# Two constants of a planned order: precedence for tanh, gates and evacuations, and a margin behind loads

## The chip, the cores and the metric

The kernel runs on one core of a Trainium2 chip. The metric is the device time of one execution in microseconds; the kernel before has a median of 448.25 us over 13 runs (447.63 to 455.56). A core has five engines with a queue each, which work side by side: TensorE (PE in the profile: matrix products, with PEld its weight loads), VectorE (DVE), ScalarE (ACT), GpSimd (POOL) and SyncE (SP), which here issues most of the DMAs. Each takes its instructions in the order written; one that waits holds up those behind it on the same engine.

## The reference

It is a cosine attention followed by a two-layer MLP on its output, with batch 8, 12 heads, 448 positions, head width 64, model width 768 and inner width 2048:

```python
q_n = q / (norm(q) + 1e-6);  k_n = k / (norm(k) + 1e-6)
attn = softmax(q_n @ k_n.T / tau)            # tau = 0.1
x = (attn @ v)  # heads joined: 3584 tokens x 768
h = x @ w_in                                 # 768 x 2048
g = h * sigmoid(1.702 * h)
out = g @ w_out                              # 2048 x 768
```

All inputs and the output are float32 in memory; the kernel multiplies in float16.

## The kernel before

**The work.** Attention goes by head pairs x = 0 to 47, six a batch. For a pair: q, k and v are loaded (L229, 224 KB each, issued by SP); q and k are squared (L242 on ScalarE; L241 on GpSimd for pairs 6 to 11) and summed by VectorE (L248); the norms are worked out by VectorE for a group of one, two or three pairs at once (L256–L293); GpSimd scales q and k (L314) and casts v (L330). Scaled q and k are transposed, by TensorE for batches 0 and 1 (L338, L350), by a DMA from SP for batch 2 on (L355, tile qkT). TensorE makes scores (L375, or L437 in halves for batches 0 and 1; tile sp), ScalarE their exp (L386, tile et), TensorE the attend (L401, or L454), VectorE its normalisation (L412, L415), and the result is transposed into xT: from batch 2 on by a DMA from SP (L425), before that on TensorE (L477, L487).

The MLP of a batch follows. mm1 makes 16 units of 128 inner columns (L500, six matmuls each; L530 for batch 0), each followed by a tanh on ScalarE (L510) and a gate on VectorE (L517, L542), which form g from h. mm2 (L555) works on two batches together, in seven tiles of 128 tokens by two halves of the width, 16 matmuls each, the first three tiles after the even batch and the other four after the odd one. ScalarE evacuates each half (L566, tile ost) and SP stores it (L583).

**Buffers.** Small pools tie the parts together: two score buffers in PSUM (sp), one attend buffer (a, tile avp), three for the products (mm), three for tanh (th), two for squares (sq), seven each for q and k, four for v, two for the output (ost). An operation of the plan takes a buffer and a later one frees it: a gate frees the mm and th of its unit, an evacuation the mm of its half, an exp frees sp, a reduction sq, a scaling q or k, and the second step of a normalisation a.

**The order.** It isn't written by hand. Each operation is added to a `Plan` with its engine, a planned time, a due number, the operations it follows, and the buffers it takes and frees. `order` (L71) runs a small event simulation of the engines and the DMA queues and writes the instructions in the order in which they start there. When an engine of the plan comes free it takes, among the operations that are ready (all they follow has ended) and whose buffers are free, the one with the lowest due number:

```python
heapq.heappush(ready[ops[u][0]], (ops[u][2], u))      # L149: (due, index)
```

Readiness comes first, the due number only chooses among what is ready. A DMA of the plan lands when its packets have passed at a fixed rate, and those who use it, and the buffers that it frees, are ready DMA_US + SEM_US = 1.9 + 0.1 us later (L129). Planned times of ScalarE are 0.82 us for an exp, 0.53 for a square, 0.46 for a tanh, 0.40 for an evacuation. Until 50 planned us, gaps of TensorE are filled by dummy transposes (L346).

Due numbers count in half pairs. Pair x has s = 2x from batch 1 on. Its loads are due s − 13, its squares and reductions 8 before the first pair of its group, the scalings about s − 5, qkT s − 3, scores and exps s to s + 1, attends and normalisations s + 2 and s + 3, xT s + 4. The products of batch b are spread over 12(b + 1) + 9 to 12(b + 2) + 9 (from 8 on for batch 0); a product's tanh, gate, evacuation and store carry the due number of the product. Loads keep a fixed order among themselves; all of SP's work, stores and transposes too, goes through SP's one queue. The loads of batch 2 stand behind the second weight load w_out.

Of the kernel before, what the change touches and what calls it, by code (L numbers as in the profile page):

```python
# [20 lines left out]
SEM_US = 0.1  # L21
SWITCH_US = 0.12
DMA_US = 1.9
DMA_ENGINES, DMA_PKT_US, DMA_KB_US = 16, 0.024, 0.037
MOE_FROM, MOE_LAG = 8, 9
WARM_FROM, KEEP_WARM, FILL_US, FILL_SPARE = 1.5, 50.0, 0.056, 0.3
# [2 lines left out]
def packets(n, nbytes):  # L29

    one = DMA_PKT_US + DMA_KB_US * nbytes / 1024
    return n * one / DMA_ENGINES, one


class Plan:
# [6 lines left out]
    def add(self, name, eng, us, due, emit, after=(), takes=(), frees=(), dma=None, rows=128, hold=(), turn=False):  # L42
        after = list(after) + list(hold)
        if turn:
            self.turns.append((due, len(self.turns), name))
        self.ops[name] = (eng, us, due, emit, after, takes, frees, dma, rows, hold)
# [24 lines left out]
    def order(self):  # L71

        for n, (_, _, name) in enumerate(sorted(self.turns)):
            eng, us, due, emit, after, takes, frees, *more = self.ops[name]
            takes, frees = [*takes, (("turn", n), 1)], [*frees, (("turn", n + 1), 1)]
            self.ops[name] = (eng, us, due, emit, after, takes, frees, *more)
            self.free["turn", n + 1] = 0
        self.free["turn", 0] = 1
        ops = list(self.ops.values())
        index = {n: i for i, n in enumerate(self.ops)}  # L80
        left = [len(o[4]) for o in ops]
        users = [[] for _ in ops]
        for i, o in enumerate(ops):
            for a in o[4]:
                users[index[a]].append(i)
        idle = {o[0]: 0.0 for o in ops}
        ready = {e: [] for e in idle}
        for i, o in enumerate(ops):
            if not left[i]:
                heapq.heappush(ready[o[0]], (o[2], i))  # L90

        lines, moved = {}, 0.0
        events, out, now, mode = [], [], 0.0, 128
        while True:
            for e in idle:
                held = []
                while idle[e] <= now and ready[e]:
                    due, i = heapq.heappop(ready[e])
                    _, us, _, emit, _, takes, _, dma, rows, _ = ops[i]
                    if any(self.free[s] < k for s, k in takes):  # L100
                        held.append((due, i))
                        continue
                    for s, k in takes:
                        self.free[s] -= k
                    out.append((now, i, emit))
                    if e == "PE" and rows != mode:
                        mode = rows
                        us += SWITCH_US
                    idle[e] = now + us
                    heapq.heappush(events, (idle[e], i, True))  # L110
                    if dma is None:
                        heapq.heappush(events, (idle[e] + SEM_US, i, False))
                for h in held:
                    heapq.heappush(ready[e], h)
            if len(out) == len(ops):
                return out

            while True:
                heads = [q[0] for q in lines.values() if q]
                total = sum(h[1] for h in heads)  # L120
                landed = min((moved + h[0] * total / h[1] for h in heads), default=None)
                if landed is None or (events and events[0][0] <= landed):
                    break
                for h in heads:
                    h[0] -= (landed - moved) * h[1] / total
                moved = landed
                for q in lines.values():
                    if q and q[0][0] <= 1e-6:
                        heapq.heappush(events, (moved + DMA_US + SEM_US, q.pop(0)[2], False))  # L129
            if not events:  # L130
                raise RuntimeError("the plan cannot go on")
            now = events[0][0]
            for h in heads:
                h[0] -= (now - moved) * h[1] / total
            moved = now
            while events and events[0][0] <= now:
                _, i, own = heapq.heappop(events)
                eng, dma = ops[i][0], ops[i][7]
                if own and dma is not None:
                    lines.setdefault(eng, []).append([*dma, i])  # L140
                for s, k in ops[i][6]:
                    if own == (s == "port" or s[0] == "turn"):
                        self.free[s] += k
                for u in users[i]:
                    if (ops[u][0] == eng and dma is None) != own:
                        continue
                    left[u] -= 1
                    if not left[u]:
                        heapq.heappush(ready[ops[u][0]], (ops[u][2], u))  # L149
# [3 lines left out]
def kernel(  # L153
# [453 lines left out]
    add = plan.add  # L607
# [10 lines left out]
    for x in range(NPAIR):  # L618
# [3 lines left out]
        for ti, nm in ((1, "k"), (0, "q")):  # L622
            add(("load", nm, x), "ACT" if x + ti == 0 else "SP", 0.5, s - 13, partial(load, x, (q32, k32)[ti], (q, k)[ti], nm + "32"),
                takes=[(nm, 1)], dma=PAIR, hold=hold, turn=True)
            pl = sq_pool(x, ti)
            add(("sq", ti, x), "POOL" if pl else "ACT", 1.0 if pl else 0.53, early + ti * 0.1, partial(square, x, ti),
                after=[("load", nm, x)], takes=[("sq", 1), ("port", int(pl))], frees=[("port", int(pl))])
            add(("red", ti, x), "DVE", 0.6, early + 0.2, partial(reduce, x, ti),
                after=[("sq", ti, x)], frees=[("sq", 1)])
# [3 lines left out]
                after=[("norm", 1, grp)], takes=[("qks", 1), ("port", 1)], frees=[(nm, 1), ("port", 1)])  # L633
        if x == grp[0]:
            reds = [("red", ti, y) for y in grp for ti in range(2)]
            n = len(grp)
# [3 lines left out]
        if x == grp[0] and not first:  # L640
# [3 lines left out]
            takes=[("v", 1)], dma=PAIR, hold=hold, turn=True)  # L644
        ca = x in CA
        add(("cast", x), "ACT" if ca else "POOL", 0.64 if ca else 0.75, s - 0.5, partial(cast_v, x),
            after=[("load", "v", x)], takes=[("vt", 1), ("port", 1 - ca)], frees=[("v", 1), ("port", 1 - ca)])
        if x < TURN:
            add(("tp", x), "PE", 0.4, s - 3, partial(transposes, x),
                after=[("scale", 0, x), ("scale", 1, x)], takes=[("a", 1), ("qkT", 1)], frees=[("qks", 2)])  # L650
            add(("qkT", x), "DVE", 0.6, s - 3, partial(transposed, x), after=[("tp", x)], frees=[("a", 1)])
        else:
            add(("qkT", x), "SP", 1.3, s - 3, partial(dma_transposed, x),
                after=[("scale", 0, x), ("scale", 1, x)], takes=[("qkT", 1)], frees=[("qks", 2)],
                dma=packets(2 * P, C * D * 4))
        if x < HALF:
            for h in range(2):
                sh = x + HP * h if first else s + h
                for u in range(2):
                    key = (x, h, u)  # L660
                    add(("s",) + key, "PE", 0.2, sh, partial(scores_h, *key), after=[("qkT", x)] + [("s", min(x + AHEAD, HP - 1), 0, 1)] * (first and h),
                        takes=[("sp", 1)], frees=[("qkT", h * u)], rows=64)
                    add(("exp",) + key, "ACT", 0.82, sh + 0.1, partial(exp, *key), after=[("s",) + key],
                        takes=[("exp", 1)], frees=[("sp", 1)])
                es = [("exp", x, h, u) for u in range(2)] + [("cast", x)]
                add(("at", x, h), "PE", 0.48, sh + 1, partial(attend_h, x, h), after=es,
                    takes=[("mm", 1)], frees=[("exp", 2), ("vt", h)])
                add(("nx", x, h), "DVE", 0.65, sh + 1, partial(normalise_h, x, h), after=[("at", x, h)],
                    takes=[("xs", 1)])
                add(("turn", x, h), "PE", 0.15, sh + 1, partial(turn_h, x, h), after=[("nx", x, h)],  # L670
                    frees=[("xs", 1)])
                add(("x", x, h), "ACT" if x in XA and not h else "DVE", 0.35, sh + 1, partial(turned_h, x, h), after=[("turn", x, h)],
                    takes=[("x", 1 - h)], frees=[("mm", 1)])
            continue
        for c in range(C):
            add(("s", x, c), "PE", 0.19, s + c // 2, partial(scores, x, c), after=[("qkT", x)],
                takes=[("sp", 1)], frees=[("qkT", int(c == C - 1))], rows=64)
            add(("exp", x, c), "ACT", 0.82, s + c // 2 + 0.1, partial(exp, x, c),
                after=[("s", x, c)], takes=[("exp", 1)], frees=[("sp", 1)])
        for j in range(2):  # L680
            es = [("exp", x, c) for c in range(C)] + [("cast", x)]
            if j == 1:
                es.append(("nx", x, 0))
            add(("at", x, j), "PE", 0.475, s + 2 + j, partial(attend, x, j), after=es,
                takes=[("a", 1)], frees=[("exp", 4 * j), ("vt", j)])
            add(("nx", x, j), "DVE", 0.55, s + 2 + j, partial(normalise, x, j), after=[("at", x, j)],
                takes=[("xf", 1 - j)], frees=[("a", 1)])
        add(("x", x), "SP", 1.0, s + 4, partial(turn, x), after=[("nx", x, 1)],
            takes=[("x", 1)], frees=[("xf", 1)], dma=packets(256, 512))
# [5 lines left out]
    def moe_due(b):  # L695
        return 2 * HP * (b + 1) + MOE_LAG if b else MOE_FROM
# [4 lines left out]
    for b in range(B):  # L701
# [3 lines left out]
        for u in units:  # L705
            key = u if b else u + ("h",)
            m, half = u[1], not b
            after = [prev] if prev else []
# [13 lines left out]
        for t in tiles:  # L722
            for n in range(2):
                for part in range(4):
                    if b:
                        after = [("g", b, 4 * part + 3)]
                    else:
                        after = [("g", h, 4 * part + 2, "h") for h in range(1 + (t > 0))]
# [18 lines left out]
    for name, us, emit, after, takes, frees, tail in moe:  # L747
        b, part = divmod(B * done / total, 1)
        start, end = moe_due(b), moe_due(b + 1)
        due = start + (end - start) * part  # L750
        done += us
        add(name, "PE", us, due, emit, after=after, takes=takes, frees=frees)
        prev = name
        for kind, eng, n, e, tk, fr in tail:
            if eng == "SP":
                add(kind + name[1:], eng, 0.5, due, e, after=[prev], frees=fr, dma=n)
            else:
                me = (kind,) + name[1:]
                before = [prev]
                if kind == "ost":  # L760
                    me = me[:-1]
                    if me[-1]:
                        before.append(me[:-1] + (0,))
                add(me, eng, n, due, e, after=before, takes=tk, frees=fr)
                prev = me
    for i in range(2):
        add(("w_in", i), "POOL", 1.0, i - 2, partial(load_w_in, i), hold=[("load", "q", HP - 2)],
# [53 lines left out]
```

## Time and profile before

| | |
|---|---|
| median of the runs | 448.25 us |
| the profiled execution: time, span | 447.82 us, 445.7 us |
| TensorE busy (share of the span) | 427.5 us (96%) |
| ScalarE busy | 301.6 us (68%) |
| VectorE busy | 236.8 us (53%) |
| GpSimd busy | 146.2 us (33%) |
| exps L386, 192 | 166.2 us on ScalarE, 35.9 idle before them |
| tanhs L510, 128 | 69.3 us, 32.6 idle before them |
| evacuations L566, 56 | 27.4 us, 43.5 idle before them |
| squares L242, 84 | 53.1 us, 25.7 idle before them |
| gates L517 and L542, 128 | 77.8 us on VectorE |

The page is one execution on the chip. Busy times are sums over the span, so a share says little of a single stage; the stretches of 20 us are read for that. A line of the timeline gives start, length, engine, line, operation, output and inputs, the count of instructions merged into it, and in brackets the idle time of the engine before it with what ended that. Records of ScalarE that follow each other overlap: two exps of 0.92 us take 1.72 together. The ends of matmuls are modelled, so a TensorE that reads as busy may still be slower than it could be; what it costs is better read from one start to the next. Small gaps on an engine that others do not wait for cost nothing.

### The profile page before, as it was taken

Reading aid. Unit: us, or ns where it says so; the run is one execution under the profiler, and the core shown is the slowest. Engines: PE = TensorE matmul, PEld = TensorE weight load, DVE = VectorE, ACT = ScalarE, POOL = GpSimd, SP = SyncE. Lnnn points to the kernel's source line nnn. Section 1 sums busy time; section 2 is a strip of 40 time slices with the busy share of each in tenths; the row PEclk is TensorE's granted clock in tenths of the full one; section 3 lists DMA queues with packets and bytes.
Section 4 is the critical chain, followed back from the end, with each engine's and each line's share of the span. In section 5 each row is a group of like instructions: output and inputs, shape, how many; then the busy total and the mean of one; then the engine's idle time right before and its main releaser. Section 6 shows DMA issues by size and latency. Waiting matters only on the chain.

```text
span 445.7 us, 10624 instructions
## 1 busy us (share of the span) xinstructions
PE 427.5 (96%) x4208; PEld 264.3 (59%) x4208; DVE 236.8 (53%) x629; ACT 301.6 (68%) x478; POOL 146.2 (33%) x209
## 2 busy tenths in 40 slices
PE   8899999898989998999999999999999999999996
PEld 8668878454545654556555654556555655565563
DVE  4857878677697527652776228651453125504400
ACT  5898398769997759876886658865775557314411
POOL 2746776287564622433150613333110000000000
PEclk9999999999999999999999999999999999999999
DMA  8999597999999996656644795536201331021022
GB/s 214 243 223 256 98 208 180 272 268 232 223 244 202 191 223 114 165 150 169 176 113 127 191 186 135 161 97 122 69 19 26 76 84 25 13 71 37 0 72 71
DMA packets 95888, 63.99 MB, mean 144 GB/s; under 512 B 56288, under 2 KB 90848, under 8 KB 95840
## 3 DMA queue, kind: packets, MB, share of 16 engines
q1 hardware_dynamic: 91952, 56.81, 53.9%
q0 software_dynamic: 3648, 6.29, 7.8%
q8 instruction: 33, 0.54, 0.5%
q10 hardware_dynamic: 240, 0.23, 0.1%
q14 instruction: 15, 0.12, 0.1%
HBM read 45.61 MB, written 11.01 MB: 127 GB/s over the span
## 4 chain that ended last, share of the span: by engine, by line
PE 69%; ACT 9%; DVE 8%; DMA 5%; issue 3%; POOL 3%; SPq 2%; ACTq 0%; POOLq 0%
PE mm L555 27%; PE mm L500 24%; PE avp L401 6%; DMA k<-in_k_dram 5%; PE sp L375 5%; ACT et L386 5%; PE tps L346 4%; ACT sq L242 2%; DVE n L248 2%; POOL qks L314 2%; SPq L583 1%; PE sp L437 1%; PE mm L454 1%; ACT th L510 1%; PE mm L530 1%
## 5 line engine op out<-in xcount | busy, mean ns | idle before, releaser
L386 ACT ACTIVATE et<-sp 112x896 f16<-112x896 f32 x192 | 166.2, 917 | 35.9 <-PE sp L375 28.1
L555 PE MATMUL mm<-w_out,gT 128*128 128x384 f16 x896 | 153.3, 326 | 0.2 <-ACT ost L566 0.2
L500 PE MATMUL mm<-xT,w_in 128*128 128x448 f16 x672 | 134.8, 353 | 1.1 <-DVE gT L517 0.9
L555 PEld LDWEIGHTS <-gT 128*128 128x128 f16 x896 | 84.4, 98 | 65.9 <-issue 13.1
L500 PEld LDWEIGHTS <-w_in 128*128 128x128 f16 x672 | 62.7, 98 | 67.6 <-issue 13.8
L517 DVE SCALAR_TENSOR_TENSOR gT<-th,mm 128x448 f16<-128x448 f16 x112 | 68.3, 616 | 56.0 <-ACT th L510 55.8
L510 ACT ACTIVATE th<-mm 128x448 f16<-128x448 f32 x128 | 69.3, 549 | 32.6 <-PE mm L500 26.5
L248 DVE TENSOR_REDUCE n<-sq 112x8 f32<-112x512 f32 x96 | 64.1, 680 | 46.4 <-ACT sq L242 45.5
L330 POOL CAST vt<-v 112x256 f16<-112x256 f32 x92 | 35.1, 402 | 119.1 <-PE avp L401 85.5
L566 ACT ACTIVATE ost<-mm 128x384 f32<-128x384 f32 x56 | 27.4, 489 | 43.5 <-PE mm L555 42.0
L314 POOL TENSOR_TENSOR qks<-k,y 112x512 f16<-112x512 f32 x42 | 43.8, 1042 | 39.1 <-DVE y L289 26.5
L401 PEld LDWEIGHTS <-et 112*128 112x128 f16 x1152 | 44.6, 97 | 15.6 <-ACT et L386 2.0
L401 PE MATMUL avp<-vt,et 112*128 112x65 f16 x1152 | 47.4, 193 | 3.1 <-ACT et L386 1.7
L314 POOL TENSOR_TENSOR qks<-q,y 112x512 f16<-112x512 f32 x42 | 43.8, 1042 | 3.5 <-DVE y L289 3.5
L412 DVE RECIPROCAL rcx<-avp 128x4 f32<-128x4 f32 x72 | 12.9, 179 | 59.4 <-PE avp L401 59.1
L375 PE MATMUL sp<-qkT 64*128 64x448 f16 x288 | 40.8, 355 | 2.0 <-ACT et L386 1.9
L242 ACT ACTIVATE sq<-k 112x512 f32<-112x512 f32 x42 | 26.5, 632 | 21.4 <-DMA k<-in_k_dram 20.7
L415 DVE TENSOR_TENSOR xf<-avp,rcx 128x256 f16<-128x256 f32 x72 | 30.6, 424 | 2.5
L242 ACT ACTIVATE sq<-q 112x512 f32<-112x512 f32 x42 | 26.6, 638 | 4.3 <-DMA q<-in_q_dram 2.9
L346 PE MATMUL tps<-ident 128*128 128x128 f16 x288 | 20.8, 234 | 4.2 <-DVE qkT L350 2.8
L346 PEld LDWEIGHTS <-ident 128*128 128x128 f16 x288 | 18.8, 106 | 5.8 <-issue 4.4
L530 PE MATMUL mm<-xT,w_in 128*128 128x224 f16 x192 | 20.7, 259 | 0.1
(44 smaller groups left out, 212.7 us busy)
## 6 DMA issues: line engine op xcount, KB each, us to landing
k<-in_k_dram SPq DMA_DIRECT2D x48, 224.0 KB, 4.6
v<-in_v_dram SPq DMA_DIRECT2D x48, 224.0 KB, 4.7
q<-in_q_dram SPq DMA_DIRECT2D x47, 224.0 KB, 5.0
w_in<-in_moe_w_in_dram POOLq DMA_DIRECT2D x2, 1536.0 KB, 16.7
w_out<-in_moe_w_out_dram POOLq DMA_DIRECT2D x2, 1536.0 KB, 14.3
out_dram<-ost SPq DMA_DIRECT2D x7, 336.0 KB, 2.8
out_dram<-ost SPq DMA_DIRECT2D x8, 288.0 KB, 2.7
out_dram<-ost SPq DMA_DIRECT2D x8, 240.0 KB, 3.0
```

Of the source, the lines that this page charges most:

```text
L242: return nc.scalar.activation(out=sqs[x, ti], in_=src, func=AF.Square)
L248: nc.vector.tensor_reduce(out=n2s[grp][:, x - grp[0], ti], in_=sqs.pop((x, ti)), axis=AX.X, op=ALU.add,)
L314: return eng.tensor_tensor(out=qkss[x][:, 1 - ti].rearrange("p c j d -> p j c d"), in0=src, in1=rss[x][:, ti, :, :, None].to_broadcast((P, ...
L330: copy(out=vt[:, :, j, :D], in_=src[:, j]) for j in range(2)
L346: nc.tensor.transpose(out=tps0[:, 2 * S : 2 * S + 128], in_=ident, identity=ident)
L375: nc.tensor.matmul(out=sp[:, j, :S], lhsT=keys(x, j, c), rhs=queries(x, j, 0, S), start=True, stop=True,)
L386: nc.scalar.activation(out=e[:, : 2 * S].rearrange("p (j s) -> p j s", j=2), in_=sps.pop(key)[:P, :, :S], func=AF.Exp, scale=inv_tau, **kw,)
L401: nc.tensor.matmul(out=ps[:, (D + 1) * t : (D + 1) * (t + 1)], lhsT=exps[x, c][:, q0 : q0 + 128], rhs=values(x, c, D * j, D * j + D + 1), ...
L500: nc.tensor.matmul(out=ps[:, :S], lhsT=w_in_sb[:, kk, 128 * m : 128 * (m + 1)], rhs=xTs[b, kk][:, :S], start=(kk == 0), stop=(kk == KT1 - 1),)
L510: nc.scalar.activation(out=ths[key], in_=mms[key][:, :S], func=AF.Tanh, scale=0.851)
L517: nc.vector.scalar_tensor_tensor(out=gts[b // 2][:, m, (b % 2) * S : (b % 2 + 1) * S], in0=ths.pop((b, m)), scalar=1.0, in1=mms.pop((b, m) ...
L555: nc.tensor.matmul(out=mms[b2, t, n][:, :NW], lhsT=gts[b2][:, kk, 128 * t : 128 * (t + 1)], rhs=w_out_sb[:, kk, NW * n : NW * (n + 1)], st ...
```

## The change

A constant line is added, and two places use it:

```diff
+LATE_FROM, LATE_US, URGENT = 80.0, 2.0, 12
...
                     if q and q[0][0] <= 1e-6:
-                        heapq.heappush(events, (moved + DMA_US + SEM_US, q.pop(0)[2], False))
+                        at = moved + DMA_US + SEM_US + LATE_US * (moved > LATE_FROM)
+                        heapq.heappush(events, (at, q.pop(0)[2], False))
...
-                add(me, eng, n, due, e, after=before, takes=tk, frees=fr)
+                add(me, eng, n, due - URGENT, e, after=before, takes=tk, frees=fr)
```

The first: a DMA whose packets have passed after 80 planned us, a load, a transpose or a store, is taken to be usable 2 us later than so far. That changes the planned time only, and with it the place of its users in their queues; the waits on the chip stay those of the data. The second: tanh, gate and evacuation (`me` in the loop over the tails of the products) get a due number lower by 12, the width of one batch, for all batches. The due numbers of the products and of the stores stay as they are. No instruction is added, removed or changed in size.

## The prediction

> **What bounds the kernel now.** I read the chain of waits first, to learn which engine sets the end and to get its prices.
>
> ```profile
> 187.35 0.49 PE avp L401 x16
> 386.78 15.60 PE mm L555 x96
> 402.38 18.16 PE mm L500 x96
> 420.54 20.81 PE mm L555 x128
> ```
>
> TensorE sets the end, and where it is fed without a break it has fixed prices: mm2 20.81/128 = 0.163 us a matmul, mm1 18.16/96 = 0.189, attend 0.49/16 = 0.031. In the timeline, scores (L375) take about 0.48 per four and 0.30 per two up to the next matmul; I use 0.13 each. Next, the busy times by 20 us stretch say where it is not fed.
>
> ```profile
> core 0: us, PE busy (x) PEld busy (x) DVE busy (x) ACT busy (x) POOL busy (x), PEclk, DMA share, GB/s
> 80.00:100.00 20.00, 17.49 (x137) 9.72 (x137) 14.68 (x41) 13.89 (x24) 11.21 (x18) 1.00 1.12 268
> 100.00:120.00 20.00, 18.23 (x202) 9.87 (x199) 13.71 (x38) 19.99 (x32) 13.76 (x20) 1.00 1.08 240
> 120.00:140.00 20.00, 18.39 (x194) 10.47 (x190) 17.77 (x49) 19.08 (x32) 7.85 (x11) 1.00 1.02 214
> 160.00:180.00 20.00, 18.03 (x168) 10.13 (x165) 12.34 (x32) 14.14 (x24) 5.30 (x8) 1.00 0.76 156
> 260.00:280.00 20.00, 19.20 (x176) 10.61 (x174) 12.01 (x32) 15.39 (x26) 6.44 (x9) 1.00 0.65 157
> 280.00:300.00 20.00, 20.00 (x186) 11.29 (x182) 12.22 (x34) 14.73 (x24) 5.41 (x9) 1.00 0.48 129
> ```
>
> The same view for single lines gives the counts. In 280:300 they are 42 mm1, 40 mm2, 24 scores, 80 attends: 42×0.189 + 40×0.163 + 24×0.13 + 80×0.031 = 20.1 us of work in 20, so that stretch has nothing to give. In 100:120: 48×0.189 + 34×0.13 + 120×0.031 = 17.2, a loss of 2.8 us. In 120:140 (42, 20 mm2, 22, 110) 17.5, a loss of 2.5; in 160:180 (54, 16, 18, 80) 17.6, 2.4; in 260:280 (54, 22, 20, 80) 18.9, 1.1; in 80:100 I take the unbusy 2.5. **The ceiling for any order of the work after 80 us is about 11.3 us**, and the stages hit are 80–140, 160–180 and 260–280. Granted clock is 1.00 throughout.
>
> Who starves TensorE? The waits on its engine and the timeline at two of those places:
>
> ```profile
> PE sp L375 <- ACT et L386: 1.9, 3, 0.8
> PE avp L401 <- ACT et L386: 1.7, 3, 0.6
> PE mm L454 <- ACT et L386: 1.5, 2, 1.3
> ```
>
> ```profile
> 82.58 0.63 ACT L242 ACTIVATE sq<-k 112x512 f32<-112x512 f32 x1 [1.36 <-DMA k<-in_k_dram]
> 84.06 0.60 PE L454 MATMUL mm<-vt,et 112*128 112x65 f16 x14 [1.33 <-ACT et L386]
> ...
> 167.33 0.63 ACT L242 ACTIVATE sq<-k 112x512 f32<-112x512 f32 x1 [3.15 <-DMA k<-in_k_dram]
> 169.62 0.57 PE L401 MATMUL avp<-vt,et 112*128 112x65 f16 x13 [0.60 <-ACT et L386]
> ```
>
> ScalarE stood 1.36 and 3.15 us before a square whose load had not landed; the exp queued behind it came late, and TensorE waited for the exp. That is one cause. The other:
>
> ```profile
> 100.37 1.31 PE L500 MATMUL mm<-xT,w_in 128*128 128x448 f16 x6
> 101.91 1.31 PE L500 MATMUL mm<-xT,w_in 128*128 128x448 f16 x6
> ...
> 106.69 1.46 ACT L510 ACTIVATE th<-mm 128x448 f16<-128x448 f32 x3
> ```
>
> The mm1 begun at 100.37 ended near 101.7; its tanh ran at 106.69, 5 us later, behind exps and squares. All three mm buffers were held, and the next mm1 began only at 105.92, when the first gate (105.26, 0.61) had released one.
>
> **The change part by part.** No instruction is added or removed, and durations stay. Two things move.
>
> *Precedence (URGENT).* Tanh (128), gates (128) and evacuations (56) are chosen before ready exps, squares, reductions and normalisations. Stores keep their due on SP, but follow their evacuation, so may come earlier there. Queued behind an urgent instruction is everything else on ScalarE and VectorE, at 0.43 us for a tanh (next start in the timeline), 0.49 for an evacuation, 0.61 for a gate; waiting for that are attends (for exps), a second attend (it needs the single avp buffer, released by the normalise) and, through later squares, POOL's scaling and the q/k/v loads on SP that wait for those buffers.
>
> In 100–140, TensorE's two stretches lose 5.3. A tanh and its gate release 1.13 us of mm1 for 0.43 of ScalarE; four exps release about 2 us for 3.3. So putting tanh first feeds TensorE better, and the exps postponed can run beside mm2, which asks for one evacuation in 2.6 us (140–160: ScalarE busy 14.4 of 20). Against it: ScalarE is busy 39.07 of 40 there, and order creates no capacity. Bounds 0 and 5.3; I take 3.0, above half, because the timeline shows the mm buffers as the stop. In 80–100, mm waits for an evacuation twice 0.2: 0.4 gained. In 160–180, mm1 waited 0.7 for a gate at 175.95: gained.
>
> *Margin (LATE).* After 80 planned us, everything fed by a DMA is planned 2 us later: squares, casts, scores behind a transposed qkT, mm1 behind xT. The planned load is 0.5 to issue, 224 packets of 0.061 over 16 engines = 0.85, and 1.9 + 0.1: 3.35 us. The trace's landings in 80:180 and in 180:300:
>
> ```profile
> k<-in_k_dram SPq DMA_DIRECT2D x17, 224.0 KB, 4.8
> ...
> k<-in_k_dram SPq DMA_DIRECT2D x14, 224.0 KB, 3.4
> ```
>
> The Trainium skill speaks against the margin: "DMA: Bandwidth & Descriptors", in its anatomy of one DMA, fits a transfer as about 2.0 us plus its bytes at 436 GB/s (a fit for GpSimd's path), an estimate of 2.5 us for 224 KB. By that the plan already waits long enough and the margin brings 0. By the row it is 1.45 us short in 80–180, and the square at 167.33 shows the price. I go by the row: 1.33 gained at 82–84, 1.2 at 168–170 (0.63 + 0.60), 0.8 at 260–280 (ScalarE waits of 2.65, 2.42 and 1.76 for k there): 3.3. ScalarE's other waits for loads, most of its 20.7 us for k, lie beside a full TensorE and give nothing.
>
> The margin has a price. Transposes landed in a median of 4.8 (qkT) and 3.5 us (xT) in 80:180, 2.6 and 2.4 later, against planned 4.15 and 3.7: for them it is mostly too much. xT has a lag that hides it. qkT has none when batch 2 starts (first scores at 97.51; ScalarE idle 1.24 before its first exp): scores placed up to 2 us later leave ScalarE idle just before its full stage. Bounds 0 and 2; I take 1.0, as mm1 of batch 1 can fill for TensorE. SP issues in planned order, so later squares and scales also move qkT transposes behind loads; one pair of transposes held SP for 10.3 us at 168.47. This may help or hurt by under 1; I take 0.
>
> New waits: 16 tanhs lie in 97–143. If each made TensorE wait its 0.43 for an exp it would be 6.9; if none, 0. Mm1 is ready during most of them: I take 1.5. From 181 to 250 and 272 to 386 TensorE is full; reordering costs nothing there while mm1 or mm2 covers it, 0.43 a place where it doesn't. Splitting a four of scores into two twos would cost 2×0.30 − 0.48 = 0.12: zero taken, up to 2 for 16 more. Before 80 us only precedence acts, on batch 0; TensorE is full in 60–80 and partly kept warm by dummy transposes before: 0, within ±1.
>
> **Sum:** 3.0 + 0.4 + 0.7 + 3.3 − 1.0 − 1.5 = 4.9 us. The profiled execution took 447.82 (span 445.7 and 2.1 around it), 0.43 below the median of 448.25. I forecast 448.25 − 4.8 = **443.5**.
>
> **The rivals.**
> 1. *The order cuts deeper.* TensorE never starves after 97: three quarters of 11.3, 8.5, gives 439.8. For it: mm work was ready in every starved stretch. Against: ScalarE's 39.07 of 40. Chance 0.16.
> 2. *No change.* ScalarE's capacity in 100–140 decides, priorities apply only where several things are ready at once, and what is won at loads returns as late exps: 448. For it: ScalarE's share; two score buffers and two square buffers keep its ready list short. Chance 0.12.
> 3. *Slower.* In 97–143, tanhs and gates push exps and normalises back, and the margin starts batch 2's scores 2 us late; ScalarE, full, can't recover either. Price 2.0 + 16×0.43 = 8.9, against 6.0 gained elsewhere (0.4 + 0.7 + 3.3, and 1.6 of the 3.0): +2.9, 451.1. It decides once TensorE waits for the postponed exps at more than about 9 of the 16 tanhs. VectorE's 17.77 of 20 in 120:140 speaks for it; mm2 as a filler against. Chance 0.22.
>
> **How the numbers follow.** The main case has 0.50 (441 to 446.5: in 100–140 the full 5.3 at the low end, 0 at the high one). About 0.2% (0.9 us) is what a measurement can tell from no change. Faster 0.50 + 0.16 = 0.66, same 0.12, slower 0.22. A range of 438.5 to 450.5 leaves out the far halves of rivals 1 and 3.
>
> **What would show it.** Right: ScalarE's wait for k below 10 us; tanh within 1.5 us of its mm1 in 97–140 and the mm1s of batch 1 finished before 130 instead of 135; TensorE over 19 busy in 100:120, 120:140 and 160:180; the last three groups of the chain unchanged in length, only earlier by 4 to 5 us. Wrong: "avp <- ACT et" or "sp <- ACT et" above 4 us, first scores of batch 2 after 99, or a new unbusy stretch after 180, where nothing is forecast to move.

## The result and the profile after

The changed kernel takes 443.89 us (median of 11 runs), the one before 449.1 (48 runs, the 13 of the beginning among them): a ratio of 0.9885, 95% interval 0.9864 to 0.9905. The forecast was 443.5. The two profiled executions are closer: 447.82 and 444.67, spans 445.7 and 442.8. All readings below are of the profiles.

The busy times by stretch, with the columns shown before. The first line is 60–80 of the kernel before, the others are the changed kernel, whose program lines are 2 higher:

```profile
60.00:80.00 20.00, 20.00 (x317) 15.91 (x315) 16.68 (x48) 16.47 (x25) 11.53 (x18) 1.00 0.93 200
...
60.00:80.00 20.00, 17.66 (x259) 11.99 (x260) 15.22 (x46) 16.15 (x20) 11.72 (x13) 1.00 0.91 176
80.00:100.00 20.00, 18.45 (x207) 11.52 (x207) 17.62 (x52) 15.00 (x27) 10.37 (x18) 1.00 1.09 241
100.00:120.00 20.00, 20.00 (x179) 9.89 (x177) 13.73 (x37) 19.87 (x32) 10.52 (x15) 1.00 1.13 256
120.00:140.00 20.00, 20.00 (x221) 11.34 (x220) 15.25 (x41) 19.73 (x31) 11.36 (x16) 1.00 1.18 224
160.00:180.00 20.00, 18.17 (x156) 9.92 (x154) 13.23 (x34) 16.05 (x27) 12.34 (x16) 1.00 1.03 189
260.00:280.00 20.00, 20.00 (x182) 11.20 (x182) 12.51 (x33) 16.17 (x26) 6.89 (x9) 1.00 0.71 165
```

TensorE is full in 100–140 and in 260–280, as forecast; ScalarE is no less busy there than before. 160–180 is hardly better, and 60–80, which was full, is not. ScalarE's waits for k (total, times, longest) fell below the forecast 10 us, before and after:

```profile
ACT sq L242 <- DMA k<-in_k_dram: 20.7, 17, 3.2
...
ACT sq L244 <- DMA k<-in_k_dram: 7.3, 6, 2.5
```

I counted every kernel's matmuls in each stretch and took them off at the fixed prices of the prediction (batch 0 and 1's forms in the same way, 0.105 for L530, 0.034 for L454, 0.061 for L437, dummies and other transposes 0.065); a matmul across an edge counts on both sides. What remains of a stretch is its **loss**:

| kernel | median us | ratio (95%) | 60–80 | 80–100 | 100–140 | 160–180 | 260–280 |
|---|---|---|---|---|---|---|---|
| before | 449.1 | | −0.5 | 3.3 | 5.4 | 2.4 | 1.2 |
| the change | 443.89 | 0.9885 (0.9864–0.9905) | 3.7 | 2.4 | 1.9 | 1.9 | −0.1 |
| 1 precedence only | 447.48 | 0.9969 (0.9951–0.9988) | 2.2 | 4.4* | 1.9 | 2.4 | 1.3 |
| 2 margin only | 445.81 | 0.9928 (0.9894–0.9963) | −0.4 | 1.7 | 7.4* | 0.0 | −0.1 |
| 3 precedence from batch 1 | 441.50 | 0.9838 (0.9797–0.9878) | −0.6 | 2.5 | 2.1 | 1.0 | 0.0 |
| 4 margin on loads only | 443.66 | 0.9887 (0.9846–0.9929) | 3.0 | 3.7 | 1.8 | 0.1 | −0.1 |
| 5 = 3 and 4 | 441.15 | 0.9844 (0.9795–0.9893) | −0.6 | 1.4 | 2.8 | 1.2 | 0.0 |
| 6 batch 0: tanhs only | 442.47 | 0.9870 (0.9826–0.9915) | 1.4 | 2.0 | 2.1 | 0.3 | −0.1 |
| 7 batch 0: gates only | 446.81 | 0.9961 (0.9943–0.9979) | 2.8 | 7.1* | 2.1 | 0.6 | −0.1 |
| 8 from batch 1, tanhs only | 440.60 | 0.9825 (0.9784–0.9865) | −0.6 | 1.6 | 2.7 | 0.3 | 0.1 |
| 9 from batch 1, gates only | 446.60 | 0.9937 (0.9912–0.9962) | −0.5 | 2.0 | 7.8* | 0.2 | 0.0 |
| 10 = 8, margin from the start | 440.24 | 0.9801 (0.9772–0.9829) | −0.1 | 0.1 | 1.9 | 0.1 | 0.0 |
| 11 = 8 without margin | 444.49 | 0.9892 (0.9859–0.9926) | −0.4 | 1.8 | 2.6 | 2.1 | 1.2 |
| 12 = 8, margin 4 us | 440.07 | 0.9800 (0.9769–0.9830) | −0.5 | 2.0 | 2.2 | 0.0 | 0.0 |

(* the granted clock was below 1 in part of it; see the last section. Runs 1–4, 5–8 and 9–12 were timed in three groups, each beside runs of the kernel before, with medians of 448.47, 448.90 and 449.19. Between groups the ratios compare better than the medians.)

The profile's difference closes on this table. From 80 to 380 the losses fell from 12.0 to 6.4 in all (5.6 gained), and there are 34 dummy transposes fewer (2.2 gained); 60–80 lost 4.2 and the first 60 us 0.6 more. That makes 3.0, against spans that differ by 2.9. The chain of waits ends as before, with groups of the same length, 3.2 earlier:

```profile
383.62 15.60 PE mm L557 x96
399.22 18.16 PE mm L502 x96
417.38 20.82 PE mm L557 x128
```

The medians differ by 2 us more than the profiles. The granted clock may explain part. Averaged over the span it was 1.000 in before's profiled execution, and 0.996 in the middle one of 71 later runs; of those, the 22 at 0.998 or more have a median of 448.4 us, the 48 at 0.996 or less one of 449.0. The change's 0.997 is no loss: it fell at 440.54, after the last matmul (438.18). So some 0.6 is accounted for, and the rest stays open.

### The profile page after: what moved, and what is told of

The parts are those of the page before. It is cut to its first block, busy times and chain, and to the rows that moved or that the text cites. A ratio compares the mean times of both kernels' runs of the same rounds, so it can differ in the third digit from the quotient of the medians.

```text
span 442.8 us, 10584 instructions
## 1 busy us (share of the span) xinstructions
PE 426.6 (96%) x4174; PEld 262.6 (59%) x4174; DVE 240.6 (54%) x629; ACT 302.0 (68%) x478; POOL 146.1 (33%) x209
## 4 chain that ended last, share of the span: by engine, by line
PE 78%; DMA 8%; DVE 5%; ACT 3%; POOL 3%; issue 2%; SPq 1%; POOLq 0%; ACTq 0%
PE mm L557 30%; PE mm L502 28%; PE sp L377 7%; PE avp L403 7%; DMA k<-in_k_dram 4%; DMA w_in<-in_moe_w_in_dram 3%; PE mm L532 2%; POOL qks L316 2%; ACT et L388 2%; DMA qkT<-qks 1%; PE mm L456 1%; DVE n L250 1%; ACT sq L244 1%; PE sp L439 1%; DVE gT L544 1%
## 5 line engine op out<-in xcount | busy, mean ns | idle before, releaser
L348 PE MATMUL tps<-ident 128*128 128x128 f16 x254 | 19.5, 239 | 3.2 <-DVE qkT L352 1.8
L348 PEld LDWEIGHTS <-ident 128*128 128x128 f16 x254 | 17.4, 109 | 4.7 <-issue 3.3
```

The costliest lines, as they stand in the source:

```text
L348: nc.tensor.transpose(out=tps0[:, 2 * S : 2 * S + 128], in_=ident, identity=ident)
```

## The experiments

**1. Precedence alone.** `LATE_US` 2.0 → 0.0.

> Precedence alone, the margin set to 0 us. Theory A (precedence frees the product buffers in 100 to 140 us, the margin unblocks squares): TensorE keeps its gain in 100-140 (loss against its fixed prices about 2 us instead of 5.4), ScalarE's wait for k is back near 20 us, and the stretches at 80-100 and around 260-280 lose 1 us each again: about 445.5 us, ratio 0.992. Theory B (the margin does all, since ScalarE is full in 100-140 and order creates no capacity): 449 us, ratio 1.000.

Measured 447.48. 100–140 keeps its gain, so theory B falls; ScalarE's wait for k is 26.6 us, and 160–180 and 260–280 lose as before. It is 2 us slower than forecast, because 60–80 loses 2.2 and 80–100 more than before.

**2. The margin alone.** `URGENT` 12 → 0.

> The margin alone, no precedence. Theory A: the loss of 5.4 us in 100-140 is back, the one around 260-280 (1.2 us) stays gone, ScalarE's wait for k stays below 10 us, and 60-80 us loses nothing: about 447.5 us, ratio 0.996. Theory B (the margin does all): 444 us, ratio 0.9885.

Measured 445.81. The losses of 160–180 and 260–280 are gone, ScalarE's wait for k is 3.1 us, and 60–80 is full. The loss in 100–140 is not only back but 2.0 larger, 1.7 of it clock. So the two parts act in different stages, and the margin is worth more than I gave it.

**3. Batch 0 without precedence.**

```diff
+                first = name[-1] == "h" or name[:2] == ("mm2", 0) and name[2] < 3
-                add(me, eng, n, due - URGENT, e, after=before, takes=tk, frees=fr)
+                add(me, eng, n, due - URGENT * (not first), e, after=before, takes=tk, frees=fr)
```

> Both parts, but batch 0's tanhs, gates and evacuations without precedence. Theory A (the new loss of 3.7 us in 60-80 comes from batch 0's urgent gates, which hold up the copies of transposed q and k and the norms of batch 1 on VectorE): that loss goes, some 2 us of dummy transposes come back, and the rest stays: about 442 us, ratio 0.985. Theory B (the start is bound by loads and weights, and what is won there is lost again in the stage with ScalarE full): 444 us, ratio 0.9885.

Measured 441.50, and TensorE in 60–80 is full again:

```profile
60.00:80.00 20.00, 20.00 (x319) 16.14 (x316) 16.98 (x49) 16.72 (x24) 11.80 (x19) 1.00 0.94 196
```

Theory A's number holds: precedence on batch 0 costs 2.4 us by the medians. What of it does so is asked in runs 6 and 7.

**4. The margin for loads only.** `LATE_US * (moved > LATE_FROM and names[i][0] == "load")`, with `names` the list of operations.

> Precedence as in the change, the margin for loads of q, k, v and weights only, none for transposes and stores. Theory A (only loads were planned too early; transposes landed as planned): the same as the change or up to 1 us faster, since scores of batch 2 need not be placed 2 us late: 443 to 444 us, ratio 0.987. Theory B (the margin acts through the transposes: scores and mm1 placed later on TensorE and less waiting in SP's queue): back to the time of precedence alone, some 445.5 us, ratio 0.992.

Measured 443.66, no different from the change. The gain of the margin lies in the loads, and leaving it off the transposes neither loses nor saves anything measurable.

**5. Both of these together.**

> The two runs before put together: precedence from batch 1 on, margin for loads only. Theory A (the two savings lie in different stages and add up: no loss in 60-80, and no loss in 160-180 as with the margin for loads only): about 440.5 us, ratio 0.982. Theory B (what the margin on transposes orders at 160-180 is luck of one plan, so with another start of the plan nothing adds): as with precedence from batch 1 on, 441.5 to 442 us, ratio 0.984 to 0.985.

Measured 441.15, not told apart from 3, and between the times of the two theories. The loss of 0.1 in 160–180 did not carry over (1.2), which speaks for theory B, that what is left there belongs to one plan's order.

**6 and 7. Which operation of batch 0 hurts.** `not first or kind == "th"`, and the same with `"g"`, in place of `not first`.

> The change, but of batch 0 only the tanhs have precedence; its gates and evacuations have none. Theory A (batch 0's urgent gates hold VectorE, which makes the copies of transposed q and k for batch 1): nothing is lost in 60-80, about 441.5 us. Theory C (whatever releases mm buffers sooner lets mm1 of batch 0 run into 40-60, and then 60-80 has no filler; the tanh is the one that releases): the loss of 3 to 4 us in 60-80 stays, about 444 us.

> The change, but of batch 0 only the gates have precedence. Theory A (VectorE): 60-80 loses 3 to 4 us as with the change, about 444 us, and more mm1 of batch 0 than before lies in 40-60. Theory C (the tanh is the one that releases): no loss in 60-80, about 441.5 us.

Measured 442.47 and 446.81. The gates move the mm1s: with gates first, 144 matmuls of batch 0's mm1 lie in 40–60 and 12 in 60–80; with the tanhs first 93 and 66; before 96 and 62. So 60–80 lacks the filler that ran too early, as theory C had it, but what releases it in batch 0 is VectorE's gate. The gates also cost more there: against run 3, 60–80 loses 3.4 us more with gates first and 2.0 more with tanhs first. 1.1 of those 2.0 is a single wait of TensorE for VectorE, which had a norm in hand. By the time run 6 can't be told apart from run 3 or from the change.

Run 7 is also slower than the change, because an attend waited 2.1 us for an evacuation in 80–100, and the clock fell. Evacuations have no precedence there; but they have none in runs 3 and 6 either, where such a wait is at most 0.5. So the lack alone does not make it, and what in this plan does is not shown.

**8 and 9. Which operation brings the gain later.** `not first and kind == "th"`, and with `"g"`.

> Margin as in the change; precedence from batch 1 on for tanhs only, gates and evacuations without. Theory A (an mm buffer waited for its tanh, behind exps and squares on ScalarE): the gain in 100-140 stays, loss there about 2 us, and the time is near that of full precedence from batch 1 on, 441.5 to 442.5 us. Rival (tanh first only moves the queue to the gate on VectorE, 17.8 of 20 us busy in 120-140 before): the loss in 100-140 is back at 5 us or more, about 445 us.

> Margin as in the change; precedence from batch 1 on for gates only. Theory A (the mm buffers waited for the tanh): the loss in 100-140 is back at 5 to 7 us, as with the margin alone, and the time is near that one's, 445 to 446 us, ratio 0.993. Rival (tanh and gate each shorten the hold, either is enough): loss in 100-140 near 2.5 us, 441.5 us.

Measured 440.60 and 446.60. The tanh alone does it. The stretches 100:120 and 120:140, first of run 8, then of run 9:

```profile
100.00:120.00 20.00, 19.24 (x187) 9.76 (x186) 14.05 (x37) 19.72 (x31) 12.68 (x17) 1.00 1.08 246
120.00:140.00 20.00, 19.81 (x236) 11.52 (x235) 13.33 (x38) 19.82 (x31) 9.04 (x14) 1.00 0.90 198
```

```profile
100.00:120.00 20.00, 17.57 (x189) 9.26 (x186) 13.77 (x37) 19.94 (x30) 13.46 (x18) 1.00 1.09 250
120.00:140.00 20.00, 17.54 (x181) 9.64 (x178) 14.78 (x40) 18.44 (x30) 8.73 (x13) 0.91 0.96 204
```

ScalarE is about as full in both; only what it does first differs, and TensorE gains 3.9 us of busy time. Of the 5.1 us between their losses 1.7 is clock.

**10, 11 and 12. How much margin, and from when.** All on run 8: `LATE_FROM` 0.0; `LATE_US` 0.0; `LATE_US` 4.0.

> Precedence for tanhs from batch 1 on, the margin of 2 us for every DMA from the start instead of after 80 planned us. Theory A (a margin is harmless only where other work covers it; the start waits for its loads and has none): squares, scales and first scores are planned late, 0 to 40 us loses 1 to 2 us more, about 442 us. Rival (loads land in 7 us in the first 80, so the margin helps there most): 439 us or less.

> Precedence for tanhs from batch 1 on, no margin. Theory A (margin and tanh precedence act in different stages): the gain in 100-140 stays, the losses of 2 to 3 us at 160-180 and 1.2 at 260-280 return with ScalarE's wait for k at 20 us or more: about 444.5 us, ratio 0.990. Rival (without the margin, squares planned too early stand before tanhs too, so that precedence gives nothing): 448 us, ratio 0.998.

> Precedence for tanhs from batch 1 on, the margin doubled to 4 us. Theory A (2 us covers what the plan lacks, about 1.5 us; more places scores and squares later than needed but mm1 and mm2 cover that): same within 1 us, 440 to 441.5 us. Rival (each further us of margin starts batch 2's scores later and costs ScalarE that time before its full stage): 442.5 us or more.

Measured 440.24, 444.49 and 440.07. Without the margin, 160–180 and 260–280 lose about what they lost before (2.1 and 1.2), and ScalarE waits 20.5 us for k: the margin is worth about 4 us. Doubling it costs nothing, so the rival, that each us of margin holds up batch 2, falls. From the start it costs nothing either: my theory A was wrong there, and the rival's 439 was not reached; the first 40 us lose 5.8 against 6.3, and 80–100 falls from 1.6 to 0.1. Runs 8, 10 and 12 can't be told apart; all three beat the change, by about 3.5 us.

## Why the prediction held, step by step

The time was right to 0.4 us, and both mechanisms were right, but the 0.4 is partly luck. The terms summed to 4.9 us (4.8 was then taken off). The profiles, which they were worked out from, differ by 3.0; the medians differ by 5.2, and most of those 2 us more is unexplained. By the losses, 100–140 gained 3.5 against 1.5; 80–100, 160–180 and 260–280 gained 0.9 + 0.5 + 1.3 = 2.7 against 4.4 less 1.0; the first 80 us lost 2.6 against 0; and other stretches lost 0.6 in small parts.

**100–140, precedence (+3.0, less 1.5 for new waits): 3.5, and no new waits.** In the changed kernel's timeline a tanh follows its mm1 soon:

```profile
101.41 1.31 PE L502 MATMUL mm<-xT,w_in 128*128 128x448 f16 x6
103.06 0.56 ACT L512 ACTIVATE th<-mm 128x448 f16<-128x448 f32 x1
```

0.34 us after it ends, against 5 before. For the mm1s begun in 97–140 this lag was 2.1 us in the mean and 6.3 at most before, 0.2 and 0.55 in the changed kernel, and up to 13.6 in run 9, where gates alone go first. Batch 1's last tanh ran at 129.85; before, its last mm1 ended near 135. TensorE's waits for an exp after 80 come to 0.2 us in all, so the 1.5 was a price for nothing. Nor do waits hide in the loss of 1.9 that is left: from one start to the next, no matmul there takes over 0.25 us more than its price, where before nine did, by 5.4 in all. What is left lies in the steps between scores and other products, which the flat 0.13 leaves out. Rival 3, which lived on the 1.5, had no place. Rival 2 (ScalarE's capacity decides) falls with run 8, where ScalarE is busy 39.54 of 40 and TensorE still loses only 2.7. Rival 1's 439.8 was too low for the change, but the kernels with tanhs alone come near it. Run 9 shows that the gate adds nothing there.

**The margin (+3.3, less 1.0): 3 to 5 by itself.** Run 11 against run 8 gives 3.9 by the medians and 3.0 by the ratios. Run 2 recovers 1.6 in 80–100, 2.4 in 160–180 and 1.3 in 260–280; but run 11 loses no more than run 2 in 80–100, so the 1.6 need not be the margin's. The estimate from the Trainium skill's "DMA: Bandwidth & Descriptors" (anatomy of one DMA), by which the margin would bring 0, does not hold for these loads, which SP issued; the row of the landings does. The price of 1.0 for batch 2's start did not show in runs 4 and 12. Its first scores did come late, at 100.92 instead of 97.51 and past the 99 that I had named as a sign of being wrong; as TensorE is full from 100 on, the sign was badly chosen.

**160–180 (+0.7, and +1.2 of the margin's 3.3): only 0.5.** Both waits moved:

```profile
167.41 0.63 ACT L244 ACTIVATE sq<-k 112x512 f32<-112x512 f32 x1 [2.26 <-DMA k<-in_k_dram]
173.38 1.68 DVE L519 SCALAR_TENSOR_TENSOR gT<-th,mm 128x448 f16<-128x448 f16 x3
174.04 1.30 PE L502 MATMUL mm<-xT,w_in 128*128 128x448 f16 x6 [1.31 <-DVE gT L519]
```

A square still stood before a load, now with a tanh behind it; and from 170.88 to 173.46 ten VectorE instructions of a norm stood in front of three gates, whose tanhs had begun at 170.90. TensorE, with 18.17 us busy, stayed below the 19 of the forecast. Runs 2, 4, 8 and 12 lose at most 0.3 there, so it isn't the margin's fault; which detail of the order decides was not separated.

**Before 80 (0, within ±1): this step failed.** I took TensorE's full 60–80 as cover that can't be lost. But mm1 of batch 0 was that cover, and gates in front let it run into 40–60, where it displaced dummy transposes. The matmuls of mm1 in 40–60, before and after:

```profile
40.00:60.00 20.00, 9.90 (x96) 1.00 0.78 156
...
40.00:60.00 20.00, 14.72 (x144) 1.00 0.72 152
```

Then VectorE, busy with gates and a norm, copied batch 1's transposed q and k late:

```profile
57.38 2.15 DVE L263 TENSOR_SCALAR y<-n 112x32 int32<-112x32 int32 x1
60.13 0.61 DVE L544 SCALAR_TENSOR_TENSOR gT<-th,mm 128x448 f16<-128x448 f16 x1
60.66 0.62 DVE L352 COPY qkT<-tps 128x896 f16<-128x896 f16 x1
61.34 0.36 PE L439 MATMUL sp<-qkT 64*128 64x224 f16 x4 [1.26 <-DVE qkT L352]
```

Net of the dummies it is 2.0 in the profile (4.2 − 2.2) and 2.4 by run 3; the 0.6 of the first 60 us is not this precedence's, as run 3 loses 0.5 there too. How much is the missing filler and how much the late copies, no run separates. I had named the gates' cost for VectorE, but priced it in 97–143 only.

## What to carry to other kernels

In a stage where an engine is full, order still matters: first what frees the scarcest buffer of the engine that sets the end, here a 0.43 us tanh that holds one of three product buffers. Give precedence where that buffer is what stops the work, not everywhere; where an engine's filler covers a later stage, spending it early moves the hole there, and cost 2 us here. And plan a user of a transfer by the landing that the trace shows, rounded up: too late cost nothing measurable here, too early blocked an in-order queue.

## What the hardware showed that I had not expected

**The clock falls without a long idle gap.** In run 2, no single wait of TensorE in 100–140 was above 0.9 us, yet after 8 us at about two thirds busy the granted clock (the column after POOL's) dropped:

```profile
116.00:120.00 4.00, 2.74 (x40) 1.63 (x40) 2.32 (x8) 4.00 (x7) 2.58 (x6) 1.00 0.84 189
120.00:124.00 4.00, 2.50 (x40) 1.60 (x41) 3.55 (x15) 4.00 (x6) 0.44 (x1) 1.00 0.69 167
124.00:128.00 4.00, 3.53 (x29) 1.96 (x29) 2.61 (x6) 2.91 (x5) 4.00 (x4) 0.57 1.31 215
```

4 × 0.43 = 1.7 us lost there: by the trace the clock was 0.5 for 3.41 us from 124.23 on. The same dip stands in runs 1 and 9 (3.41 us at 0.5, 1.7 us lost each), and one of twice the length in run 7 (6.83 us, 3.4 lost), always in the stretch with the largest loss. So a stage that starves TensorE can pay for it nearly twice: in run 7, 3.4 of the 7.1 is clock. The Trainium skill ("TensorE: Matmul & The Clock Gate", on HAM oscillation) gives as its abstract rule no idle gap of TensorE above some 3.4 us, and adds, as a second failure mode, a kernel whose frequent micro-idles made the clock swing. Run 2 looks like this second kind. No threshold follows from these runs: before, TensorE was only 0.60 busy in 123–127 and kept the full clock, while in run 1, where no 4 us have less than 0.61, it dipped at 90.66.

**One small VectorE instruction took 2.15 us.** The norm's first step (112x32) takes 0.19 us; in the changed kernel and in runs 1, 4 and 7, those with precedence for batch 0's gates, it took 2.15 once. In the changed kernel that was from 57.38 to 59.53, while two scalings ran on GpSimd from 57.46 to 59.49, and in the other three it also lay beside two scalings. A second one, begun at 69.85 beside one scaling, took 0.68 and again ended 0.04 us after it. In the other runs none took more than 0.9. That GpSimd held it up is argued from these times, not tested.
